# Group 0's first loads reordered and split: q first, k in two parts, key tiles cast and transposed apart, at the start of a fused attention and feed-forward kernel

## The chip, the cores and the metric

The kernel runs on one core of one Trainium2 chip. The metric is the device time of one execution in microseconds (us), the median of several runs; lower is better. Engines are named as the profile names them: PE is TensorE (matmuls; PEld are its weight loads), ACT is ScalarE, DVE is VectorE, POOL is GpSimd and SP is SyncE. POOL and SP issue the transfers (DMAs) between the chip's main memory and on-chip memory in this kernel.

## The reference

Two stages follow each other. The first is attention with a sigmoid in place of the softmax, for 8 batches of 12 heads, 448 tokens and a head size of 64. The second is a feed-forward layer with a Swish gate that has a learned slope for each hidden unit.

```python
def _attn_ref(q, k, v):                      # each (8, 12, 448, 64), float32
    S = q.shape[2]
    scale = 1.0 / np.sqrt(q.shape[-1])
    scores = scale * np.matmul(q, k.transpose(0, 1, 3, 2)) - np.log(S)
    attn = 1.0 / (1.0 + np.exp(-scores))
    return np.matmul(attn, v).astype(np.float32)

x = attn_out.transpose(0, 2, 1, 3).reshape(B * S, H * D)     # (3584, 768)

def _moe_ref(x, w_in, w_out, beta):          # w_in (768, 2048), w_out (2048, 768)
    h = x @ w_in
    g = h * (1.0 / (1.0 + np.exp(-beta * h)))
    return (g @ w_out).astype(np.float32)
```

## The kernel before

All matmuls take 16-bit operands. Heads are taken in groups of four; a batch has three groups (0, 1 and 2 make up the first batch). A group's q and k are loaded with the tokens on 128 partitions as four heads of 32 rows, and DVE's stream transposes turn them into `qT` and `kT`. A head's 448 keys fall into four key tiles: tiles 0, 1 and 2 of 128 keys and tile 3, the last, of 64.

A **visit** (`half_visit`) computes scores of one group for half of the queries (224). PE writes them to two score tiles in PSUM, and ACT turns each of the two into sigmoid weights with one instruction (`weigh`, L242). There are two kinds of visit. The first kind (`second` is 0) takes key tiles 0 and 1, and both of its score tiles are 896 wide. The second kind takes key tile 2 for all heads and then key tile 3; one of its score tiles is 896 wide, and the other, the narrow one, 448. A visit has 16 matmuls at L229; four that use different rows of the array start together. Three pairs of PSUM banks hold score tiles in turn, so a visit waits until ACT has weighed what was in its pair before. `attend` ("values", L332) multiplies the weights with v, and DVE copies the result to `xT` (L341). The first layer (`dense1`, L354) multiplies `xT` with `w_in`; ACT and DVE apply the gate (L366, L369). A unit of it is one matmul; the first 48 units take half-width operands of 224 columns, six units to each of the 16 column blocks of `w_in`, and the units behind them include full ones of 448.

All instructions stand in an order that is written out by hand. For the beginning, the list `BEGIN` holds that order: visits (`"scores"`, group, half, kind), transposes (`"k"`, `"q"`), values, units of the first layer (`"dense"`), and rows of filler matmuls (`"idle"`, L812) that multiply a tile of zeros and write to a bank that nobody reads. Each engine takes its own share of the list strictly in this order.

Two queues load the first data. SP issues group 0's k and the first half of its q, in 32-bit form, into a staging area (L787), and then `beta`. The staged parts are cast to 16 bits: k's first 8 of 14 chunks by DVE (L798), the other 6 and q by ACT (L796). POOL issues all other loads (L125, L154, L169, L177), which cast while they move: group 1's q, group 1's k, group 2's k and q, four parts of v, the other halves of q, and then `w_in` in eight parts, in the order of the list `LOADS`. From its ninth load on, a load of POOL waits until the one eight places before it has landed.

In `BEGIN`, group 0 starts like this: all of k cast, q cast, all of k transposed in two instructions (L212), q transposed (L200), group 1's q transposed, 20 fillers, the visit of the second kind, 4 fillers, the visit of the first kind. The two transposes of k cover all its key tiles: one takes row blocks 0 and 1 (four key tiles), the other row blocks 2 and 3 (three key tiles).

Of the kernel before, what the change touches and what calls it, by code (L numbers as in the profile page):

```python
# [9 lines left out]
FP16 = mybir.dt.float16  # L10
# [3 lines left out]
def kernel(  # L14
# [42 lines left out]
    kTp = ctx.enter_context(tc.tile_pool(name="kTp", bufs=3))  # L57
# [60 lines left out]
    raws = {}  # L118
# [64 lines left out]
    kT = {}  # L183
    at_tiles = {}
    xTs = {}
    ready = set()


    def in_order(b: int, t):
        t = t.rearrange("p c e -> p (c e)").bitcast(FP32)  # L190
        return t.rearrange("p (q c) -> p c q", c=NB) if b == B - 1 else t

    def transpose(g: int, r: int, c0: int = 0, c1: int = NB):
        raw = raws[g][:, r]
        assert g or (r, c0) == (0, NB // 2) or all((r, "cast", c) in ready for c in range(c0, c1))
        if r == 0:
            if g not in qT:
                qT[g] = qTp.tile([P, NB * BLK, PAIR], FP16, tag="qT", name="qT")
            ready.update((g, "q", c) for c in range(c0, c1, NB // 2))
            nc.vector.transpose(  # L200
                out=in_order(g // QPB, qT[g][:, c0 * BLK : c1 * BLK]),
                in_=raw[:, c0:c1].rearrange("p c d -> p (c d)").bitcast(FP32),
            )
            return
        ready.add((g, "k"))
        kT[g] = kTp.tile([P, S, PAIR], FP16, tag="kT", name="kT")
        to = kT[g].rearrange("p k e -> p (k e)").bitcast(FP32)
        frm = raw.rearrange("p c d -> p (c d)").bitcast(FP32).rearrange("p (c f) -> p c f", c=NB)
        half = to.rearrange("p (x i q) -> p x i q", i=2, q=BLK)
        for i in (0, 2):  # L210
            c, n = rows_of(i)
            nc.vector.transpose(  # L212
                out=half[:, i // 2 :: 2].rearrange("p j i q -> p i j q"),
                in_=frm[:, c : c + 2 * n].rearrange("p (i j) f -> p i j f", j=n),
            )

    def score_tile():
        i, j = scored[n_sc[0] % len(scored)]
        n_sc[0] += 1
        width[i] = width[j] = S  # L220
        return ps[:, i : j + 1]

    def score(sco, u0: int, s: int, jt: int, hh: int, e: int, c0: int, n: int):
        g, lo = s // 2, (s % 2 * 2 + hh) * BLK
        assert (g, "k") in ready and all(
            (g, "q", c) in ready for c in range(c0 // BLK, (c0 + n) // BLK, NB // 2)
        )
        base, nk = (last_base(s), KL) if jt == JF else (0, P)
        nc.tensor.matmul(  # L229
            sco[base : base + nk, hh, u0 : u0 + n],  # L230
            kT[g][lo : lo + BLK, jt * P : jt * P + nk, e],
            qT[g][lo : lo + BLK, c0 : c0 + n, e],
            start=(e == 0),
            stop=(e == PAIR - 1),
            tile_position=(lo, base),
        )
# [3 lines left out]
    def weigh(sco, n: int):  # L240
        slot = at_free.pop(0)
        nc.scalar.activation(  # L242
            out=attns[:, slot, :, 0:n],
            in_=sco[:, :, 0:n],
            func=AF.Sigmoid,
            bias=nlogs[:, 0:1],
            scale=MSCALE,
        )
        return slot
# [41 lines left out]

    def half_visit(g: int, c0: int, second: int):
        slots = (2 * g, 2 * g + 1)
        scos = [score_tile() for _ in slots]
        plan = [(s, jt, sco, jt * QH) for jt in (0, 1) for s, sco in zip(slots, scos)]
        widths = [S, S]
        if second:
            plan = [(s, 2, sco, 0) for s, sco in zip(slots, scos)]
            plan += [(s, JF, scos[0], QH) for s in slots]
            widths = [S, QH]  # L300
        for i in range(0, len(plan), 2):
            for e in range(PAIR):
# [447 lines left out]
    def fill_units(n: int):  # L750
        for _ in range(n):
            fill[at_fill[0]][1]()
            at_fill[0] += 1

    NH = NB // 2
    share_psum(3)
    with tc.manual_schedule():
        def load(what, *a):
# [23 lines left out]
        ]  # L782
        staged = gt[:, 0:4].rearrange("p c w -> p (c w)").bitcast(FP32)
        raws[0] = rawp.tile([P, 2, NB, D], FP16, tag="raw", name="raw")
        parts = {1: (staged, NB), 0: (staged[:, NB * D :], NH)}
        for r, (to, n) in parts.items():
            nc.sync.dma_start(  # L787
                out=to[:, 0 : n * D],
                in_=(q, k)[r][0, 0:HQ].rearrange("h (p c) d -> (h p) (c d)", c=NB)[:, 0 : n * D],
            )  # L790

        def cast(r: int, c0: int, c1: int, act: bool):
            out = raws[0][:, r, c0:c1].rearrange("p c d -> p (c d)")
            frm = parts[r][0][:, c0 * D : c1 * D]
            if act:
                nc.scalar.copy(out=out, in_=frm)  # L796
            else:
                nc.vector.tensor_copy(out=out, in_=frm)  # L798
            ready.update((r, "cast", c) for c in range(c0, c1))

        nc.gpsimd.memset(nlogs, NEG_LOG_S)
        nc.gpsimd.memset(dummy, 0.0)
# [5 lines left out]
        idle = bank(512)  # L808
# [13 lines left out]
        def beta_columns():  # L822
# [16 lines left out]
        for what, *a in BEGIN:  # L839
            if what == "q":  # L840
                g, half = a
                transpose(g, 0, half * NH, (half + 1) * NH)
            elif what == "k":
                transpose(a[0], 1)
            elif what == "scores":
                half_visit(a[0], a[1] * QH, a[2])
            elif what == "cast":
                cast(*a)
            elif what == "idle":
                idle_units(a[0])  # L850
            elif what == "v":
                double_v_last(a[0])
            elif what == "values":
                attend(a[0], a[1] * QH, QH, a[2:] or (0, 1))
            elif what == "dense":
                fill_units(a[0])
            elif what == "beta":
                beta_columns()
            elif what == "loads":
                loads()  # L860
            elif what == "two":
                share_psum(2)
# [156 lines left out]
```

## Time and profile before

| what | value |
|---|---|
| median of 3 runs | 373.51 us (373.1 to 373.65) |
| the profiled execution | 372.95 us |
| its span, first to last instruction | 371.2 us |
| mean granted PE clock | 0.999 |
| full clock granted from | 5.40 us |
| PE busy | 365.5 us (98%) |
| ACT busy | 259.7 us (70%) |
| DVE busy | 254.4 us (69%) |
| mean busy share of the 16 DMA engines | 80% or more in the first 9 of 40 slices of the span, less behind |

The profile comes from one execution. Times in it count from its first instruction. The timeline gives the start, the duration and the engine of merged instructions, with the number of them behind an "x"; a merged row's duration reaches from the first start to the last end. Brackets tell how long the engine was idle before and what ended it. A load's landing is the time at which its semaphore tells of its end. The chain is followed back from the last instruction, at each step to what released it. These landings are read from the trace:

| load | issued | landed |
|---|---|---|
| group 0's k (SP) | 0.74 | 3.90 |
| group 0's q, first half (SP) | 1.17 | 4.46 |
| beta (SP) | 1.64 | 5.54 |
| group 1's q, first half | 1.29 | 5.97 |
| group 1's k | 2.00 | 7.21 |
| group 2's k | 2.53 | 8.45 |
| group 2's q, first half | 3.05 | 9.14 |
| v, last of four parts | 5.41 | 12.79 |
| w_in, first part | 9.43 | 16.74 |
| w_in, fourth part | 12.17 | 23.66 |

### The profile page before, as it was taken

Reading aid. Unit: us, or ns where it says so; the run is one execution under the profiler, and the core shown is the slowest. Engines: PE = TensorE matmul, PEld = TensorE weight load, DVE = VectorE, ACT = ScalarE, POOL = GpSimd, SP = SyncE. Lnnn points to the kernel's source line nnn. Section 1 sums busy time; section 2 is a strip of 40 time slices with the busy share of each in tenths; the row PEclk is TensorE's granted clock in tenths of the full one; section 3 lists DMA queues with packets and bytes.
Section 4 is the critical chain, followed back from the end, with each engine's and each line's share of the span. In section 5 each row is a group of like instructions: output and inputs, shape, how many; then the busy total and the mean of one; then the engine's idle time right before and its main releaser. Section 6 shows DMA issues by size and latency. Waiting matters only on the chain.

```text
span 371.2 us, 7295 instructions
## 1 busy us (share of the span) xinstructions
PE 365.5 (98%) x2906; PEld 184.6 (50%) x2906; DVE 254.4 (69%) x479; ACT 259.7 (70%) x311; POOL 80.5 (22%) x120
## 2 busy tenths in 40 slices
PE   8999999999999999999999999999999999999997
PEld 4566544443444455544444445554444455555665
DVE  4435796777496967787666667778767667679671
ACT  5995766798967668887877749887678647883000
POOL 7732431221131013233131003233100002230000
PEclk9999999999999999999999999999999999999999
DMA  9999999893368030029829410017803111000334
GB/s 173 195 197 204 202 205 206 193 123 51 51 86 174 1 87 1 2 49 130 171 37 212 106 25 20 3 29 110 171 2 85 44 44 42 1 2 1 87 85 129
DMA packets 36226, 34.65 MB, mean 93 GB/s; under 512 B 9424, under 2 KB 32608, under 8 KB 36192
## 3 DMA queue, kind: packets, MB, share of 16 engines
q0 software_dynamic: 30288, 22.47, 42.3%
q1 hardware_dynamic: 5904, 11.71, 11.1%
q8 instruction: 23, 0.38, 0.4%
q14 instruction: 11, 0.09, 0.1%
HBM read 45.62 MB, written 11.01 MB: 153 GB/s over the span
## 4 chain that ended last, share of the span: by engine, by line
PE 93%; ACT 5%; issue 1%; DVE 0%; ACTq 0%
PE ps L643 27%; PE ps L523 26%; PE ps L229 11%; PE ps L332 10%; PE ps L354 9%; PE ps L384 4%; PE ps L437 4%; ACT attns L242 3%; ACT attns L257 1%; PE ps L812 1%; ACT sg L366 1%; DVE gt L369 0%; ACT osb L664 0%; DVE still L806 0%; ACT osb L399 0%
## 5 line engine op out<-in xcount | busy, mean ns | idle before, releaser
L257 ACT ACTIVATE attns<-ps,nlogs 128x1792 f16<-128x1792 f32 x75 | 131.7, 1756 | 41.1 <-PE ps L229 41.0
L643 PEld LDWEIGHTS <-sum 128*128 128x128 f16 x440 | 40.5, 98 | 37.3 <-issue 12.5
L537 POOL TENSOR_TENSOR gt<-attns,sg 128x448 f16<-128x448 f32 x21 | 23.9, 1137 | 141.7 <-ACT sg L534 141.7
L229 PE MATMUL ps<-qT,kT 32*128 32x448 f16 (+3 forms) x864 | 52.3, 339 | 1.1 <-ACT attns L242 0.6
L534 ACT ACTIVATE sg<-ps,beta_sb 128x448 f32<-128x448 f32 x72 | 45.2, 632 | 8.4 <-PE ps L523 5.9
L523 PE MATMUL ps<-xT,w_in 128*128 128x448 f16 x216 | 49.2, 353 | 0.0
L523 PE MATMUL ps<-xT,w_S 128*128 128x448 f16 x216 | 49.2, 352 | 0.0
L643 PE MATMUL ps<-w_T,sum 128*128 128x384 f16 x264 | 48.7, 327 | 0.0
L537 DVE TENSOR_TENSOR gt<-ps,sg 128x448 f16<-128x448 f32 x72 | 44.2, 618 | 4.0 <-ACT sg L534 3.8
L341 DVE CAST xT<-ps 128x448 f16<-128x448 f32 (+1 forms) x54 | 28.8, 567 | 21.5 <-PE ps L332 21.5
L523 PEld LDWEIGHTS <-w_in 128*128 128x128 f16 x288 | 28.0, 98 | 26.6 <-issue 0.7
L661 DVE TENSOR_TENSOR osb<-ps,osb 128x384 f32<-128x384 f32 x55 | 30.5, 554 | 15.1 <-PE ps L643 12.8
L332 PE MATMUL ps<-attns,v 128*64 128x448 f16 (+3 forms) x432 | 40.4, 340 | 0.1
L354 PE MATMUL ps<-xT,w_in 128*128 128x448 f16 (+1 forms) x240 | 39.5, 316 | 0.6 <-DVE gt L369 0.6
L630 DVE TENSOR_TENSOR sum<-gt 128x1024 f16<-128x1024 f16 x55 | 36.5, 678 | 0.2
L369 DVE TENSOR_TENSOR gt<-ps,sg 128x448 f16<-128x448 f32 (+1 forms) x40 | 20.0, 527 | 22.4 <-ACT sg L366 22.3
L125 POOL DMA_DIRECT2D raw<-in_q_dram x26 | 14.4, 555 | 92.8 <-DVE kT L212 84.7
L643 PE MATMUL ps<-w_out,gt 128*128 128x384 f16 x176 | 33.3, 327 | 0.0
L643 PE MATMUL ps<-w_out,sum 128*128 128x384 f16 x176 | 32.3, 327 | 0.0
L583 DVE TENSOR_TENSOR ps<-ps,attns 128x448 f32<-128x448 f32 x24 | 15.2, 632 | 23.3 <-PE ps L523 19.4
L523 PEld LDWEIGHTS <-w_S 128*128 128x128 f16 x216 | 21.1, 98 | 19.4
L354 PEld LDWEIGHTS <-w_in 128*128 128x128 f16 x240 | 22.0, 98 | 16.9 <-issue 5.8
(52 smaller groups left out, 364.3 us busy)
## 6 DMA issues: line engine op xcount, KB each, us to landing
out_dram<-osb SPq DMA_DIRECT2D x100, 96.0 KB, 2.2
raw<-in_k_dram POOLq DMA_DIRECT2D x23, 224.0 KB, 5.3
raw<-in_q_dram POOLq DMA_DIRECT2D x21, 224.0 KB, 4.1
v<-in_v_dram POOLq DMA_DIRECT2D x16, 192.0 KB, 6.9
w_in<-in_moe_w_in_dram POOLq DMA_DIRECT2D x8, 384.0 KB, 11.9
w_out<-in_moe_w_out_dram POOLq DMA_DIRECT2D x4, 768.0 KB, 15.0
v<-in_v_dram POOLq DMA_DIRECT2D x16, 144.0 KB, 7.5
out_dram<-osb SPq DMA_DIRECT2D x5, 144.0 KB, 2.4
```

The source lines that it names most:

```text
L229: nc.tensor.matmul(sco[base : base + nk, hh, u0 : u0 + n], kT[g][lo : lo + BLK, jt * P : jt * P + nk, e], qT[g][lo : lo + BLK, c0 : c0 + n ...
L257: nc.scalar.activation(out=attns[:, slot : slot + 2].rearrange("p n h s -> p (n h) s"), in_=sco, func=AF.Sigmoid, bias=nlogs[:, 0:1], scal ...
L332: nc.tensor.matmul(av[hh * D : (hh + 1) * D, 0:n], vs[b][base : base + nk, 2 * (s % NPAIR) + hh, jt], at[base : base + nk, hh, 0:n], start ...
L341: nc.vector.tensor_copy(out=xTs[b][:, s % NPAIR, c0 : c0 + n], in_=av[:, 0:n])
L354: nc.tensor.matmul(m1, w_in16[:, hc, dc * P : (dc + 1) * P], xTs[b][:, hc, c0 : c0 + n], start=(hc == 0), stop=(hc == NHC - 1),)
L369: nc.vector.tensor_tensor(out=gt[:, dc, off : off + n], in0=m1, in1=sg[:, 0:n], op=ALU.mult)
L523: nc.tensor.matmul(out, w[:, c, i * P : (i + 1) * P], m[:, c], start=(start and c == 0), stop=(c == KH - 1), skip_group_check=not start,)
L534: nc.scalar.activation(out=sg, in_=h, func=AF.Sigmoid, bias=0.0, scale=beta_sb[:, dc : dc + 1])
L537: return lambda: engine.tensor_tensor(out=gt[:, dc, b % 2 * S : b % 2 * S + S], in0=h, in1=sg, op=ALU.mult)
L630: nc.vector.tensor_tensor(out=sums[t, i], in0=x, in1=y, op=op)
L643: nc.tensor.matmul(m2, (x if op is None else sums[t, i])[:, dc], w[:, dc], start=first, stop=(dc == ND - 1), skip_group_check=i >= 4,)
L661: nc.vector.tensor_tensor(out=out, in0=in0, in1=in1, op=op)
```

## The change

SP issues three loads for group 0 in place of two: the half of q first, then k's first 8 chunks, then its other 6. The casts follow key tiles: `cast_q` takes q (on ACT), and `cast_k(i, lo, hi, act)` takes key tiles `lo` to `hi` of row blocks `i` and `i + 1`. `transpose` takes a range of key tiles for k, and the score matmuls ask for their key tile only. In `BEGIN`, q is cast and transposed first; then key tiles 2 and 3 are cast (the part from k's first load by DVE, the small part from its second load by ACT) and transposed; then come 16 fillers and the visit of the second kind; then key tiles 0 and 1 are cast (by DVE) and transposed, and the visit of the first kind follows without a filler between.

A visit's `second` may be 2: its two score tiles swap places, and ACT weighs the narrow one first. This holds for group 0's and group 2's first visits of the second kind.

Rows of fillers change: 16, 11 in three rows, 8, 9 and 4 (48 in all) for 20, 4, 2, 2, 8 and 6 (42). Group 1's q is transposed between the ks of groups 1 and 2. On POOL's queue, the second half of group 2's q moves behind three parts of `w_in`. Rows of the first layer between the visits become 9, 6, 21 and 12 units for 12, 6, 21 and 9, so that the fourth part of `w_in` is first used behind group 2's visit instead of ahead of it.

```diff
-    def transpose(g: int, r: int, c0: int = 0, c1: int = NB):
+    def transpose(g: int, r: int, c0: int = 0, c1: int = NB, tiles=(0, JF + 1)):
...
-        kT[g] = kTp.tile([P, S, PAIR], FP16, tag="kT", name="kT")
+        if g not in kT:
+            kT[g] = kTp.tile([P, S, PAIR], FP16, tag="kT", name="kT")
...
         for i in (0, 2):
             c, n = rows_of(i)
+            lo, hi = tiles[0], min(tiles[1], n)
             nc.vector.transpose(
-                out=half[:, i // 2 :: 2].rearrange("p j i q -> p i j q"),
-                in_=frm[:, c : c + 2 * n].rearrange("p (i j) f -> p i j f", j=n),
+                out=half[:, 2 * lo + i // 2 : 2 * hi - 1 + i // 2 : 2].rearrange("p j i q -> p i j q"),
+                in_=frm[:, c : c + 2 * n].rearrange("p (i j) f -> p i j f", j=n)[:, :, lo:hi],
             )
...
-        scos = [score_tile() for _ in slots]
+        scos = [score_tile() for _ in slots][:: -1 if second == 2 else 1]
...
-            ats = {id(sco): weigh(sco, n) for sco, n in zip(scos, widths)}
+            order = list(zip(scos, widths))[:: -1 if second == 2 else 1]
+            ats = {id(sco): weigh(sco, n) for sco, n in order}
...
         LOADS = [
-            ("q", 1, 0), ("k", 1), ("k", 2), ("q", 2, 0), ("v", 0, 3), ("q", 1, 1), ("q", 0, 1),
-            ("q", 2, 1), ("w_in", 0, 2), ("w_in", 2, 4), ("w_in", 4, 6), ("w_in", 6, 8), ("w_in", 8, 10),
-            ("w_in", 10, 12), ("w_in", 14, 16), ("w_in", 12, 14),
+            ("q", 1, 0), ("k", 1), ("k", 2), ("q", 2, 0), ("v", 0, 3), ("q", 1, 1), ("q", 0, 1), ("w_in", 0, 2),
+            ("w_in", 2, 4), ("w_in", 4, 6), ("q", 2, 1), ("w_in", 6, 8), ("w_in", 8, 10), ("w_in", 10, 12),
+            ("w_in", 14, 16), ("w_in", 12, 14),
         ]
...
-        parts = {1: (staged, NB), 0: (staged[:, NB * D :], NH)}
-        for r, (to, n) in parts.items():
+        parts = {1: staged, 0: staged[:, NB * D :]}
+        cut = 2 * rows_of(0)[1]
+        for r, c0, c1 in ((0, 0, NH), (1, 0, cut), (1, cut, NB)):
             nc.sync.dma_start(
-                out=to[:, 0 : n * D],
-                in_=(q, k)[r][0, 0:HQ].rearrange("h (p c) d -> (h p) (c d)", c=NB)[:, 0 : n * D],
+                out=parts[r][:, c0 * D : c1 * D],
+                in_=(q, k)[r][0, 0:HQ].rearrange("h (p c) d -> (h p) (c d)", c=NB)[:, c0 * D : c1 * D],
             )
...
+        def cast_k(i: int, lo: int, hi: int, act: bool):
+            c, n = rows_of(i)
+            out = raws[0][:, 1, c : c + 2 * n].rearrange("p (i j) d -> p i j d", j=n)
+            frm = parts[1][:, c * D : (c + 2 * n) * D].rearrange("p (i j d) -> p i j d", j=n, d=D)
+            copied(out[:, :, lo:hi], frm[:, :, lo:hi], act)
...
         BEGIN = [
-            ("cast", 1, 0, 8, False), ("cast", 1, 8, 14, True), ("cast", 0, 0, 7, True), ("k", 0), ("q", 0, 0),
-            ("q", 1, 0), ("idle", 20), ("scores", 0, 0, 1), ("idle", 4), ("scores", 0, 0, 0), ("k", 1),
-            ("idle", 2), ("k", 2), ("q", 2, 0), ("idle", 2), ("scores", 1, 0, 0), ("beta",), ("idle", 8),
-            ("scores", 1, 0, 1), ("v", 0), ("idle", 6), ("scores", 2, 0, 0), ("values", 0, 0), ("q", 1, 1),
-            ("scores", 2, 0, 1), ("q", 0, 1), ("values", 1, 0), ("scores", 0, 1, 0),
-            ("values", 2, 0), ("scores", 0, 1, 1), ("dense", 12), ("scores", 1, 1, 1), ("two",), ("dense", 6),
-            ("scores", 1, 1, 0), ("loads",), ("q", 2, 1), ("dense", 21), ("scores", 2, 1, 0), ("dense", 9),
-            ("values", 0, 1), ("scores", 2, 1, 1), ("values", 1, 1), ("values", 2, 1), ("dense", 39), ("k", 3),
-            ("q", 3, 0), ("q", 3, 1), ("dense", 45),
+            ("cq", 0, 7, True), ("q", 0, 0), ("ck", 0, 2, 4, False), ("ck", 2, 2, 3, True), ("k", 0, 2, 4),
+            ("idle", 16), ("scores", 0, 0, 2), ("ck", 2, 0, 2, False), ("ck", 0, 0, 2, False), ("k", 0, 0, 2),
+            ("scores", 0, 0, 0), ("k", 1), ("idle", 4), ("idle", 4), ("q", 1, 0), ("k", 2), ("idle", 3),
+            ("scores", 1, 0, 0), ("q", 2, 0), ("idle", 8), ("scores", 1, 0, 1), ("beta",), ("idle", 9),
+            ("v", 0), ("scores", 2, 0, 0), ("idle", 4), ("values", 0, 0), ("q", 1, 1), ("scores", 2, 0, 2),
+            ("q", 0, 1), ("values", 1, 0), ("scores", 0, 1, 0), ("values", 2, 0), ("scores", 0, 1, 1),
+            ("dense", 9), ("scores", 1, 1, 1), ("two",), ("dense", 6), ("scores", 1, 1, 0), ("loads",),
+            ("q", 2, 1), ("dense", 21), ("scores", 2, 1, 0), ("dense", 12), ("values", 0, 1),
+            ("scores", 2, 1, 1), ("values", 1, 1), ("values", 2, 1), ("dense", 39), ("k", 3), ("q", 3, 0),
+            ("q", 3, 1), ("dense", 45),
         ]
```

More of the change, by code (lines that the diff above doesn't have):

```diff
@@ L191, in in_order @@
         return t.rearrange("p (q c) -> p c q", c=NB) if b == B - 1 else t
-    def transpose(g: int, r: int, c0: int = 0, c1: int = NB):
+    def transpose(g: int, r: int, c0: int = 0, c1: int = NB, tiles=(0, JF + 1)):
         raw = raws[g][:, r]
-        assert g or (r, c0) == (0, NB // 2) or all((r, "cast", c) in ready for c in range(c0, c1))
+        assert g or r == 1 or c0 or all((r, "cast", c) in ready for c in range(c0, c1))
         if r == 0:
@@ L204, in transpose @@
             return
-        ready.add((g, "k"))
-        kT[g] = kTp.tile([P, S, PAIR], FP16, tag="kT", name="kT")
+        if g not in kT:
+            kT[g] = kTp.tile([P, S, PAIR], FP16, tag="kT", name="kT")
+        ready.update((g, "k", j) for j in range(*tiles))
         to = kT[g].rearrange("p k e -> p (k e)").bitcast(FP32)
@@ L211, in transpose @@
             c, n = rows_of(i)
+            lo, hi = tiles[0], min(tiles[1], n)
+            assert g or all((1, "cast", i, j) in ready for j in range(lo, hi))
             nc.vector.transpose(
-                out=half[:, i // 2 :: 2].rearrange("p j i q -> p i j q"),
-                in_=frm[:, c : c + 2 * n].rearrange("p (i j) f -> p i j f", j=n),
+                out=half[:, 2 * lo + i // 2 : 2 * hi - 1 + i // 2 : 2].rearrange("p j i q -> p i j q"),
+                in_=frm[:, c : c + 2 * n].rearrange("p (i j) f -> p i j f", j=n)[:, :, lo:hi],
             )
@@ L224, in score @@
         g, lo = s // 2, (s % 2 * 2 + hh) * BLK
-        assert (g, "k") in ready and all(
+        assert (g, "k", jt) in ready and all(
             (g, "q", c) in ready for c in range(c0 // BLK, (c0 + n) // BLK, NB // 2)
@@ L784, with copied @@
         raws[0] = rawp.tile([P, 2, NB, D], FP16, tag="raw", name="raw")
-        parts = {1: (staged, NB), 0: (staged[:, NB * D :], NH)}
-        for r, (to, n) in parts.items():
+        parts = {1: staged, 0: staged[:, NB * D :]}
+        cut = 2 * rows_of(0)[1]
+        for r, c0, c1 in ((0, 0, NH), (1, 0, cut), (1, cut, NB)):
             nc.sync.dma_start(
-                out=to[:, 0 : n * D],
-                in_=(q, k)[r][0, 0:HQ].rearrange("h (p c) d -> (h p) (c d)", c=NB)[:, 0 : n * D],
-            )
-        def cast(r: int, c0: int, c1: int, act: bool):
-            out = raws[0][:, r, c0:c1].rearrange("p c d -> p (c d)")
-            frm = parts[r][0][:, c0 * D : c1 * D]
+                out=parts[r][:, c0 * D : c1 * D],
+                in_=(q, k)[r][0, 0:HQ].rearrange("h (p c) d -> (h p) (c d)", c=NB)[:, c0 * D : c1 * D],
+            )
+        def copied(out, frm, act: bool):
             if act:
@@ L798, in cast, with cast_q @@
                 nc.vector.tensor_copy(out=out, in_=frm)
-            ready.update((r, "cast", c) for c in range(c0, c1))
+        def cast_q(c0: int, c1: int, act: bool):
+            out = raws[0][:, 0, c0:c1].rearrange("p c d -> p (c d)")
+            copied(out, parts[0][:, c0 * D : c1 * D], act)
+            ready.update((0, "cast", c) for c in range(c0, c1))
+        def cast_k(i: int, lo: int, hi: int, act: bool):
[3 more added lines that the diff above has]
+            copied(out[:, :, lo:hi], frm[:, :, lo:hi], act)
+            ready.update((1, "cast", i, j) for j in range(lo, hi))
         nc.gpsimd.memset(nlogs, NEG_LOG_S)
@@ L843 @@
             elif what == "k":
-                transpose(a[0], 1)
+                transpose(a[0], 1, tiles=tuple(a[1:]) or (0, JF + 1))
             elif what == "scores":
                 half_visit(a[0], a[1] * QH, a[2])
-            elif what == "cast":
-                cast(*a)
+            elif what == "cq":
+                cast_q(*a)
+            elif what == "ck":
+                cast_k(*a)
             elif what == "idle":
```

## The prediction

> **What bounds the kernel now.** The page comes first: the groups of engines, then the chain that ended last.
>
> ```profile
> PE 365.5 (98%) x2906; PEld 184.6 (50%) x2906; DVE 254.4 (69%) x479; ACT 259.7 (70%) x311; POOL 80.5 (22%) x120
> PE 93%; ACT 5%; issue 1%; DVE 0%; ACTq 0%
> ```
>
> TensorE (PE) carries 93% of the chain, ScalarE (ACT) 5%. The change touches only the beginning, so I asked for busy time in three stretches.
>
> ```profile
> core 0: us, PE busy (x) PEld busy (x) DVE busy (x) ACT busy (x) POOL busy (x), PEclk, DMA share, GB/s
> 0.00:6.30 6.30, 5.11 (x37) 3.27 (x38) 2.25 (x7) 2.56 (x4) 5.14 (x15) 1.00 0.74 168
> 6.30:29.50 23.20, 21.65 (x343) 14.16 (x343) 10.16 (x32) 22.38 (x30) 12.27 (x17) 1.00 1.42 194
> 29.50:371.20 341.70, 338.71 (x2532) 167.14 (x2528) 242.01 (x441) 234.71 (x277) 63.13 (x89) 1.00 0.48 85
> ```
>
> From 6.3 to 29.5 us ACT is busy 22.38 of 23.20 us: its sigmoids on scores pace that stretch, and PE's busy time there holds 22 filler matmuls. After 29.5 PE never idles for more than 0.07 us at once (gaps of 0.17 us in all). So what reaches PE's first full-width matmul of the first layer (at 29.48) earlier ends the kernel earlier by as much, if its loads are there. The start in order of time, by the timeline:
>
> ```profile
> 0.74 0.38 SPq L787 DMA_DIRECT2D gt<-in_k_dram  x1
> 1.17 0.42 SPq L787 DMA_DIRECT2D gt<-in_q_dram  x1
> 1.19 4.39 PE L812 MATMUL ps<-still 128*128 128x256 f16 x20 [1.19 <-DVE still L806]
> 3.92 1.13 ACT L796 CAST raw<-gt 128x384 f16<-128x384 f32 x2 [1.69 <-DMA gt<-in_k_dram]
> 3.92 0.56 DVE L798 CAST raw<-gt 128x512 f16<-128x512 f32 x1 [2.66 <-DMA gt<-in_k_dram]
> 4.51 0.70 DVE L212 STREAM_TRANSPOSE kT<-raw 128x256 f32<-128x256 f32 x2
> 5.14 0.37 DVE L200 STREAM_TRANSPOSE qT<-raw 128x224 f32<-128x224 f32 x1
> 5.56 0.70 PE L229 MATMUL ps<-qT,kT 32*128 32x224 f16 x16
> 6.32 13.59 ACT L242 ACTIVATE attns<-ps,nlogs 128x896 f16<-128x896 f32 x16 [1.27 <-PE ps L229]
> 7.23 0.71 DVE L212 STREAM_TRANSPOSE kT<-raw 128x256 f32<-128x256 f32 x2 [0.82 <-DMA raw<-in_k_dram]
> 13.08 0.99 PE L332 MATMUL ps<-attns,v 128*64 128x224 f16 x16
> ```
>
> k lands, is cast, transposed, then q is transposed last, PE scores, and ACT begins at 6.32. It runs nearly without a gap from there.
>
> **The start, step by step.** Group 0's bytes stay the same (672 KB in three loads for two), so the last part of k lands about when the last load lands now: q, at 4.46. I take 4.5. Bounds: 4.2, and 4.9 if a third load costs as much as a third issue (0.42). q alone should land between 3.0 (the 192 KB store takes 3.0 from issue, a 128 KB one 1.8) and 3.9 (k's 448 KB); its cast (0.57, the 448-wide one) and transpose (0.37) are done by 4.9 even at 3.9, so q leaves the path. Behind k's last part:
> - ACT's cast of 128x128: rows of 384 and 448 take 0.512 and 0.566 us, so about 0.30 (bounds 0.2 and 0.51).
> - DVE's transpose of one key tile, 128x64: 0.20 (bounds 0.15; 0.34 of the 192-wide).
> - two hand-overs of about 0.03: 4.50 + 0.02 + 0.30 + 0.03 + 0.20 + 0.04 = 5.09 for PE's first score, against 5.56.
> - The first narrow tile needs 8 matmuls, not 16. At the warm spacing (four start together, 0.1 us apart) they take 0.3; at the slow clock, at which they may still run, 0.45. ACT starts at 5.09 + 0.45 + 0.02 = 5.56, against 6.32: **0.76 earlier**.
>
> ACT then needs 0.68 for the narrow tile and 0.91 for each wide one (start to start in the trace). The remaining casts (two of 256 wide, 0.3 to 0.4 each) and transposes (0.25 each) of tiles 0 and 1 are DVE work behind the first one; they end at 6.0 to 6.4, PE scores until 6.9, ACT is busy until 5.56 + 0.68 + 0.91 = 7.15. Hidden, with 0.25 to spare. That is also what weighing the narrow tile first buys: it covers the second half of its own visit.
>
> **Where the gain meets loads.** Next visit: group 1's k lands at 7.21 as before (nothing ahead of it on POOL's queue changes). Transposes 0.63, q's 0.41 (now between the two ks; its load landed at 5.97), so PE scores from 8.29 to 8.80. ACT is free at 7.15 + 2 x 0.91 = 8.97: still 0.73 earlier than 9.70. Group 2's k lands at 8.45 and its q is transposed by 9.6, scored first at 11.7: no wait. Fillers rise from 42 to 48 in number, but each row behind the first stands before a visit that waits for a load or for ACT anyway; PE's fourth and fifth visits are ready at 10.70 and 12.30, ACT free at 10.78 and 12.37.
>
> Then `values(0, 0)` needs all four parts of v. The last lands at 12.79, 0.29 us before its use at 13.08 now. With the change PE is there at 12.83, so it starts at about 12.87. From here PE's chain is on the path: 0.91 for values, 0.63 for the next visit's issue, 0.91 for `values(1, 0)` and 0.51 + 0.02 for the visit after: ACT goes on at 15.84, against 16.50. **0.66 is left.** The later ACT work up to the last narrow tile is the same eight short sigmoids and the same visits, only moved by three units of the first layer; I cost that at nothing.
>
> One more load is near: w_in's fourth part lands at 23.66, and its first use is PE's unit 37. Before, that stood ahead of group 2's last first-kind visit, at about 23.8; the change puts the visit first, and the unit would start at 23.78. So q's second half of group 2, moved behind three w_in loads on POOL's queue (these land about 0.58 earlier, 112 KB at 194 GB/s), costs nothing: it lands near 20.5 and is transposed at 21.7. `beta` lands some 0.4 later than 5.54 and is wanted after 9.4.
>
> Sum on the profiled execution: 372.95 (span 371.20, 1.75 around it) - 0.65 = 372.30. That execution lies 0.56 below the median of the runs shown, 373.51.
>
> **The clock, weighed.** The first 20 fillers take 4.39 us (0.22 each); 8 later ones take 1.05 (0.13 each), and the trace grants full clock from 5.40 us on. The change shortens the first row to 16 fillers, ending near 4.8, and leaves PE idle for some 0.3 us before its scores. If the full clock comes in a run at 6 to 7.5 us instead of 5.40, the first visit of before runs slow: three steps of 0.1 us between its groups of four double, 0.3 later, of which ACT's small later waits (0.06, 0.05, 0.06) take up half, so it loses 0.15. The change's first visit is already priced slow. So over runs with such a spread the gain is 0.65 to 0.8. I take 0.75: 373.51 - 0.75 = 372.75. The Trainium skill ("TensorE: Matmul & The Clock Gate", Part 1) says that the full clock follows a busy window of about 3.4 us whose phase is free-running. The trace agrees as far as it goes: one grant, 4.2 us after the first filler. By that rule 16 fillers (3.5 us) fill such a window only in some phases, which speaks against this change and is the second rival.
>
> **Rivals.**
> 1. *Loads cap it.* Both margins behind the 0.66 are about 0.1 us. If v's last part or w_in's fourth lands later by 0.3 us, the gain is 0.65 - 0.2 to 0.3 = 0.4; by 0.6, nothing to 0.2. For it: DMA share 1.42 in this stretch, every load queued, k's cut adding packets. Against: the same bytes in the same order ahead of v. Time 373.1 to 373.5.
> 2. *PE stays at the slow clock; slower than before.* Price: while the clock is half, PE's work from 8.3 us on (visits, values, fillers, with hardly any idle) takes twice as long, so a grant at T loses about (T - 8.3)/2, less the 0.65. Even at 8.8 us; over 0.75 us lost from 11 us; at 12.2 us 1.95 - 0.65 = 1.3 lost: 374.8. For it: the shorter first row, and PE's idle stretch of 0.2 to 0.3 us before 8.29, after 11 fillers, which waits for group 1's k. Against: PE idles only about 0.3 us of the 4.2 us before 5.40, and in the trace of before idle stretches of 0.37 and 0.27 us (7.0, 8.7) did not lose the clock.
> 3. *The order isn't kept*: a third load lands last at 5.0 or the small copies cost their upper bounds (0.51, 0.34 and 0.4 us): PE at 5.6, ACT at 6.1, gain 0.2 to 0.3: 373.2. It counts with the first.
>
> **How the numbers follow.** A measurement of this kernel tells 0.2% (0.75 us) from no change. My forecast, the earlier start passed on to the end, has a chance of 0.65; its centre stands at that bound, and runs with a late clock are on the far side of it, so 0.50 faster and 0.15 within. Rivals 1 and 3 together 0.15, within. Rival 2 has 0.20: 0.18 slower, 0.02 within. Faster 0.50, same 0.32, slower 0.18. The range: below, the whole 0.76, the 0.3 of a slow first visit and 0.3 of measuring (half the 0.55 between the runs shown), 372.1; above, rival 2 with a grant just past 11 us, 374.2. It leaves out some 0.15 of rival 2 and a little below. The forecast's own range is 372.2 to 373.1.
>
> **What would show it.** Right: ACT's first sigmoid is a 448-wide one at about 5.55; ACT has no wait over 0.15 us up to 13 us; `values(0, 0)` starts within 0.1 us of v's landing; the first full-width matmul of the first layer stands near 28.85 (29.48 now); after it PE's gaps stay under 0.3 us in all. Wrong: that matmul near 29.5 with PE waiting for v or w_in (rival 1); fillers after 6 us still 0.2 us apart, or visits that take 0.9 us of PE (rival 2); the last part of k after 4.9 (rival 3).

## The result: slower by 1.0%

The changed kernel takes **377.3 us** (median of 6 runs, 376.36 to 377.84) where the kernel before takes 373.37 (6 runs, 373.1 to 373.65) on the same chip: a ratio of 1.0101, with a 95% interval of 1.009 to 1.0112. The forecast was 372.75, in a range of 372.1 to 374.2. The profiled execution of after took 377.84, with a span of 376.10, against 372.95 and 371.20 before. Ratios are worked out from all executions but those in a slower state of the chip (the eleventh of run 5, 381.91), so they are not quite the quotients of the medians.

The page of after: the engines' groups, then the chain that ended last.

```profile
PE 367.5 (98%) x2912; PEld 185.6 (49%) x2912; DVE 254.5 (68%) x483; ACT 259.4 (69%) x311; POOL 80.7 (21%) x120
PE 93%; ACT 3%; DMA 2%; issue 1%; DVE 0%; SPq 0%; ACTq 0%
```

The totals hardly move, but DMA stands in the chain with 2%, where it did not stand before. Busy time by stretch (columns as before; the first full-width matmul of the first layer is at 34.02 now, 29.48 before, and the last two stretches meet there):

```profile
core 0: us, PE busy (x) PEld busy (x) DVE busy (x) ACT busy (x) POOL busy (x), PEclk, DMA share, GB/s
0.00:6.30 6.30, 3.60 (x16) 2.26 (x16) 1.30 (x5) 2.05 (x3) 5.10 (x14) 1.00 0.66 138
6.30:34.00 27.70, 25.18 (x368) 16.23 (x368) 11.24 (x37) 22.82 (x31) 13.58 (x19) 1.00 1.38 196
34.00:376.10 342.10, 338.70 (x2532) 167.13 (x2528) 242.00 (x441) 234.48 (x277) 62.06 (x87) 1.00 0.46 83
```

The last stretch is 342.1 us long against 341.7, with the same 2532 matmuls. So of the 4.9 us that the span gained, 4.54 stand ahead of that matmul. The cause lies in the start; here is its timeline in after:

```profile
0.74 0.38 SPq L792 DMA_DIRECT2D gt<-in_q_dram  x1
1.17 0.89 SPq L792 DMA_DIRECT2D gt<-in_k_dram  x2
1.19 3.60 PE L827 MATMUL ps<-still 128*128 128x256 f16 x16 [1.19 <-DVE still L821]
3.36 0.56 ACT L799 CAST raw<-gt 128x448 f16<-128x448 f32 x1 [1.13 <-DMA gt<-in_q_dram]
...
4.58 0.31 DVE L215 STREAM_TRANSPOSE kT<-raw 128x128 f32<-128x128 f32 x1
7.84 0.30 ACT L799 CAST raw<-gt 128x128 f16<-128x128 f32 x1 [3.91 <-DMA gt<-in_k_dram]
8.17 0.25 DVE L215 STREAM_TRANSPOSE kT<-raw 128x64 f32<-128x64 f32 x1 [3.28 <-ACT raw L799]
8.47 2.23 PE L232 MATMUL ps<-qT,kT 32*128 32x224 f16 x32 [3.68 <-DVE kT L215]
9.08 3.39 ACT L245 ACTIVATE attns<-ps,nlogs 128x448 f16<-128x448 f32 x4 [0.94 <-PE ps L232]
10.63 2.53 PE L827 MATMUL ps<-still 128*128 128x256 f16 x11
13.09 0.88 PE L232 MATMUL ps<-qT,kT 32*128 32x224 f16 x16
13.91 1.05 PE L827 MATMUL ps<-still 128*128 128x256 f16 x8
14.02 3.34 ACT L245 ACTIVATE attns<-ps,nlogs 128x896 f16<-128x896 f32 x4 [1.54 <-PE ps L232]
```

Two things are to be seen. First, q and k's first part are there by 3.96 and their copies are done by 4.9 (the transpose at 4.58), but ACT's cast of k's second part waits 3.91 us for its load: it landed at 7.82. Everything of the first visit stands behind it, and the first sigmoid is at 9.08 instead of 6.32: **2.76 late**. Second, the third visit's first sigmoid is at 14.02 instead of 9.70: **another 1.56**. In between stand 11 fillers that take 2.53 us, 0.22 each; the 8 after them take 1.05, 0.13 each. The trace records the full clock from 13.80 on (from 5.40 before). The chain in order of time shows both pieces on the path (start, us, what):

```profile
1.64 6.17 DMA gt<-in_k_dram
...
8.47 2.23 PE ps L232 x29
10.70 2.46 PE ps L827 x11
13.16 0.82 PE ps L232 x16
```

From there on the lateness grows by only 0.22 up to the first layer (34.02 against 29.48).

### The profile page after: what moved, and what is told of

The parts are those of the page before. It is cut to its first block, busy times and chain, and to the rows that moved or that the text cites. A ratio compares the mean times of both kernels' runs of the same rounds, so it can differ in the third digit from the quotient of the medians.

```text
span 376.1 us, 7313 instructions
## 1 busy us (share of the span) xinstructions
PE 367.5 (98%) x2912; PEld 185.6 (49%) x2912; DVE 254.5 (68%) x483; ACT 259.4 (69%) x311; POOL 80.7 (21%) x120
## 4 chain that ended last, share of the span: by engine, by line
PE 93%; ACT 3%; DMA 2%; issue 1%; DVE 0%; SPq 0%; ACTq 0%
PE ps L647 27%; PE ps L527 25%; PE ps L232 12%; PE ps L336 10%; PE ps L358 9%; PE ps L388 4%; PE ps L441 4%; DMA gt<-in_k_dram 2%; PE ps L827 1%; ACT attns L245 1%; ACT attns L260 1%; ACT sg L370 1%; SPq L792 0%; ACT osb L668 0%; DVE gt L373 0%
## 5 line engine op out<-in xcount | busy, mean ns | idle before, releaser
L527 PEld LDWEIGHTS <-w_in 128*128 128x128 f16 x288 | 28.0, 98 | 26.6 <-issue 0.7
L232 PEld LDWEIGHTS <-kT 32*128 32x128 f16 (+1 forms) x864 | 14.8, 97 | 32.2 <-issue 25.7
```

What stands on the lines that cost most here:

```text
L232: nc.tensor.matmul(sco[base : base + nk, hh, u0 : u0 + n], kT[g][lo : lo + BLK, jt * P : jt * P + nk, e], qT[g][lo : lo + BLK, c0 : c0 + n ...
L527: nc.tensor.matmul(out, w[:, c, i * P : (i + 1) * P], m[:, c], start=(start and c == 0), stop=(c == KH - 1), skip_group_check=not start,)
```

## Experiments

Theory T: the loss begins with k's second part, which lands late because SP's third load runs beside POOL's stream of loads. The rivals were the new order of bytes (q first), the slow clock by itself, and the other edits of the change.

**1. One load for k, all else as in after.**

```diff
-        for r, c0, c1 in ((0, 0, NH), (1, 0, cut), (1, cut, NB)):
+        for r, c0, c1 in ((0, 0, NH), (1, 0, NB)):
```

> The changed kernel with group 0's k in one load behind q (two SP loads in place of three; q still first). Theory T, the tail: the changed kernel loses because k's second part (1536-byte packets, first at 3.30 us, last at 7.31) runs while POOL's packets (first at 3.24) are already on the DMA engines; with two loads all packets are issued 0.5 us sooner and k lands at 4.3 to 5.0; ACT's first sigmoid at 5.6 to 6.1; full clock by 8.9 at the latest; time 372.7 to 373.6. Rival R, the order: whichever load stands behind q is caught, so k lands at 5.5 to 8 and the time is 375 to 377.5. Rival C, the clock: k lands by 5 but 16 fillers are too few, the full clock comes at 12 us or later, and the time is 374 to 375.5.

Measured: 372.96 us, ratio 1.0001 (0.999 to 1.0012). The whole k landed at 4.50, the first score stood at 5.50 and the first sigmoid at 6.12. So q's place ahead of k costs nothing, and neither do the casts by key tile: the loss of 1% goes with the third load. The eleven runs fall into two groups, 372.67 to 372.96 (six) and 373.81 to 374.44 (five). The profiled execution, at 373.81, is of the upper one, and its timeline has the second cost of after still in it: the fillers ahead of the third visit are 0.2 us apart up to 9.34, where T had the full clock by 8.9:

```profile
7.66 2.19 PE L827 MATMUL ps<-still 128*128 128x256 f16 x11
```

**2 and 6. POOL's first load issued later.** A fill on POOL ahead of its loads, of a tile that is written over later, delays its whole queue (1.38 us of fill in run 2; in run 6 the fill is twice as wide and takes 2.66).

```diff
         nc.gpsimd.memset(dummy, 0.0)
+        nc.gpsimd.memset(w_out16[:, 0:2], 0.0)     # run 6: 0:4
```

> The changed kernel with one memset on POOL (128x1536, of a part of w_out's tile that is loaded over later) ahead of POOL's first load, so that POOL's loads begin some 1 to 2 us later. Theory T: SP's three loads then end alone, k's second part lands at 4.2 to 4.8 instead of 7.82, ACT's first sigmoid comes at 5.5 to 5.9; POOL's loads land as late as in the changed kernel or up to 0.5 us later than that, so that group 1's k and v bound instead: time 374 to 376. Rival (a third SP load is slow by itself): k's second part still lands after 6.5, time 377 to 379.

> The changed kernel with a memset of 128x3072 on POOL ahead of its first load (that of 128x1536 took 1.38 us and put POOL's first packet at 3.98; this one should put it near 5.4). Theory T: k's second part, SP's third load, is late only by running beside POOL's packets; now it runs alone and lands at 4.2 to 4.8 (7.82 in the changed kernel, 6.19 with the shorter memset). Rival: a third load on SP's queue is slow by itself, and it lands after 5.8. The time (376 to 378) tells nothing, since all of POOL's loads come later.

Measured: run 2 376.06, ratio 1.0075 (1.0062 to 1.0088); run 6 374.87 in one execution. The table has what the theory speaks of, with POOL's first packet taken from the trace's packet records.

| kernel | POOL's first packet | k's second part lands | first sigmoid | third visit's first sigmoid |
|---|---|---|---|---|
| after | 3.24 | 7.82 | 9.08 | 14.02 |
| run 2 | 3.98 | 6.19 | 7.28 | 11.79 |
| run 6 | 4.82 | 5.08 | 6.34 | 11.07 |

The later POOL's stream, the earlier the third load: 2.74 us of its lateness go with it. T had 4.2 to 4.8 for both runs. In run 2 POOL's packets still came 1.8 us ahead of the load's last one (5.82), and it landed 1.4 later than T's latest. In run 6 its last packet ends at 4.77, ahead of all of POOL's, and it still lands 0.6 later than the last load of before (4.46): that is the price, in one execution, of a third load with nothing of POOL beside it, 0.3 above what T expected at most. SP's loads in the DMA view (KB of one, us from issue to landing), of after and then of run 6:

```profile
gt<-in_k_dram SPq DMA_DIRECT2D x1, 256.0 KB, 2.8
gt<-in_q_dram SPq DMA_DIRECT2D x1, 224.0 KB, 2.6
gt<-in_k_dram SPq DMA_DIRECT2D x1, 192.0 KB, 6.2
```

```profile
...
gt<-in_k_dram SPq DMA_DIRECT2D x1, 192.0 KB, 3.4
```

The first two loads take the same in both; the third, the smallest, takes 6.2 or 3.4. The mixing costs POOL's stream too: in run 2 group 1's k lands at 8.00, against 8.80 in after, though POOL issued its loads 0.83 later. Neither run mends the kernel: PE idles until its first score, the clock is slow ahead of the third visit, and run 6 issues POOL's first loads 2.1 us later, so its time (376 to 378 was expected) is no price of the load alone.

**3. The third load from another queue.** k's second part is issued by ACT, at 0.74, ahead of its table load.

```diff
-            nc.sync.dma_start(
+            (nc.scalar if c0 else nc.sync).dma_start(
                 out=parts[r][:, c0 * D : c1 * D],
```

> The changed kernel with k's second part issued from ACT's queue (ahead of its table load) instead of as SP's third load; bytes and packets as in the changed kernel. Theory T: its packets start at about 1.8 instead of 3.30 and are done before POOL's spread; k's second part lands at 3.9 to 4.6, q up to 0.6 later than 3.34, ACT's first sigmoid at 5.4 to 5.9; time 372.5 to 373.5. Rival (the number of packets and parts costs, not the time at which they start): the last of the three loads still lands after 6.5, time 376 to 378.

Measured: 374.5, ratio 1.0032 (1.002 to 1.0044). The loads land at 4.10 (q), 4.28 (k's second part, from ACT's queue) and 4.82 (k's first part), the first sigmoid is at 6.45. The load is on time as T says, but the time is 1 us above what T expected at most. What is left grows while the clock is slow: the full one is recorded from 9.18 only, and the third visit's first sigmoid stands at 10.48, 0.78 behind before, where the first one was 0.13 behind. That the clock did it is argued from these times, not shown by this run.

**7. The cut alone, in the kernel before.** Only k's load is cut, order k, k, q; no other edit.

```diff
-        for r, (to, n) in parts.items():
+        for r, c0, c1 in ((1, 0, 8), (1, 8, NB), (0, 0, NH)):
...
```

> The kernel before with one thing of the change: k's load cut in two (8 and 6 chunks), in the order k, k, q, so that q is SP's third load. Nothing else is changed. Theory T: what comes third is caught beside POOL's packets, so q lands at 6 to 8 instead of 4.46, ACT's first sigmoid comes at 7.9 to 9.8, and the time is 375 to 377.5. Rival (q first, or the small 1536-byte packets, is what made it late): q lands by 5.0 and the time is 373.0 to 373.9.

Measured: **376.89**, ratio 1.0102 (1.0089 to 1.0116): the whole loss of after, from this one edit. Now both parts of k land early, at 3.52 and 3.97, and q, which is third, lands at 7.13. Its timeline where q arrives:

```profile
7.16 0.56 ACT L796 CAST raw<-gt 128x448 f16<-128x448 f32 x1 [2.65 <-DMA gt<-in_q_dram]
7.75 0.70 DVE L200 STREAM_TRANSPOSE qT<-raw 128x224 f32<-128x224 f32 x2 [2.83 <-ACT raw L796]
...
8.22 0.70 PE L229 MATMUL ps<-qT,kT 32*128 32x224 f16 x16 [2.58 <-DVE qT L200]
```

In both orders the load that is third on SP's queue is late, be it k's second part or q.

**4. PE kept at work until k is there.** After with 46 fillers for 16.

```diff
-            ("idle", 16), ("scores", 0, 0, 2),
+            ("idle", 46), ("scores", 0, 0, 2),
```

> The changed kernel with 46 fillers in the first row instead of 16 (PE busy with zeros until about 8.4 us). k's second part still lands near 7.8 and ACT's first sigmoid comes at 8.9 to 9.1. Theory T with the clock as its consequence: the full clock comes at 5 to 8 us instead of 13.80, the 11 fillers ahead of group 1's first visit take 1.3 instead of 2.46 us, ACT's idle stretch of 1.5 us before 14.0 goes away, and the time falls by 1.2 to 2 us against the changed kernel, to 375.3 to 376.1. Rival C (the clock is the main loss): the time falls by 3 us or more, to 374.3 or less. If the slow clock costs nothing: 377 to 377.6.

Measured: 376.43, ratio 1.0079 (1.0066 to 1.0092), 0.87 below after. The full clock is recorded from 6.74, and the 11 fillers ahead of the third visit take 1.38 where they took 2.53. k's part landed at 7.49, but the fillers ran to 9.07: the first score is at 9.01, and the first sigmoid at 9.44, 0.36 later than after's. T had expected the time to fall by 1.2 to 2 us, and it fell by less. So the slow clock cost after between 0.87 and, if the 0.36 passes to the end in full, 1.2 us; the other 2.7 to 3.1 of its 3.9 are the late load.

**11. Fewer fillers ahead of the third visit.** After with 2 in place of 4 + 4 + 3.

```diff
-            ("scores", 0, 0, 0), ("k", 1), ("idle", 4), ("idle", 4), ("q", 1, 0), ("k", 2), ("idle", 3),
+            ("scores", 0, 0, 0), ("k", 1), ("idle", 2), ("q", 1, 0), ("k", 2),
```

> The changed kernel with 2 fillers instead of 11 ahead of group 1's first visit. Theory: in the changed kernel those 11 ran at the slow clock (10.63 to 13.09 us), on the path, and made ACT's idle stretch of 1.5 us before 14.0; with 2 this stretch falls below 0.4 us and the time by 0.9 to 1.5, to 375.8 to 376.5. Rival (group 1's loads, transposes or the slow clock itself hold that visit): 376.8 to 377.8.

Measured: 376.79, ratio 1.0095 (1.0081 to 1.0109), 0.51 below after by the medians and 0.81 by the profiled executions. The third visit's first sigmoid comes forward to 12.44, by 1.58, but the clock is still slow until 14.04, and at the first full-width matmul (33.16) 0.86 is left. The theory had expected 0.9 to 1.5 at the end, to 376.5 at most; the median lies at the rival's edge (376.8). Taking fillers out wins only a part: what follows them is slow as well.

**10. The shorter first row, in the kernel before.**

```diff
-            ("q", 1, 0), ("idle", 20), ("scores", 0, 0, 1), ("idle", 4), ("scores", 0, 0, 0), ("k", 1),
+            ("q", 1, 0), ("idle", 16), ("scores", 0, 0, 1), ("idle", 4), ("scores", 0, 0, 0), ("k", 1),
```

> The kernel before with 16 fillers in the first row instead of 20 and nothing else changed. Theory (a shorter row lets the full clock come a window of 3.4 us later in part of the runs): the first score starts at 5.56 as before, but the runs spread: some at 373.1 to 373.5 and some 0.4 to 1.0 us above them, median 373.3 to 374.0. Rival (the row's length does nothing by itself; only the late load made the clock slow): 373.1 to 373.6 with no group above.

Measured: 373.94 (8 runs, 373.21 to 374.84), ratio 1.0021 (1.001 to 1.0033). Busy time and granted clock (PEclk, the value behind POOL's) in four stretches of 3.41 us between the clock changes that the trace of this run records, at 3.89, 7.30 and 14.13:

```profile
0.48:3.89 3.41, 2.70 (x13) 1.94 (x14) 0.40 (x2) 1.49 (x2) 2.73 (x7) 1.00 0.59 189
3.89:7.30 3.41, 1.92 (x27) 0.96 (x25) 1.93 (x5) 1.72 (x3) 2.81 (x5) 1.00 1.05 161
7.30:10.71 3.41, 3.04 (x38) 1.62 (x36) 2.43 (x9) 2.99 (x5) 1.89 (x4) 0.50 1.36 190
10.71:14.13 3.42, 3.42 (x29) 1.76 (x28) 0.45 (x2) 2.46 (x3) 3.39 (x6) 0.50 1.41 195
```

The full clock came at 3.89 and was taken away again at 7.30, after a stretch in which PE was busy 1.92 of 3.41 us, waiting 1.49 of it for q's transpose. (In this execution k and q landed 0.37 and 0.36 later than in that of before, which is a part of the wait.) The 0.50 of the next two stretches lasts until 14.13. The phase of these stretches is not the kernel's to choose, but over eight runs the four fillers fewer cost 0.67 us, with k's load uncut.

**5. Both repairs.** After with one load for k and 20 fillers.

```diff
-        for r, c0, c1 in ((0, 0, NH), (1, 0, cut), (1, cut, NB)):
+        for r, c0, c1 in ((0, 0, NH), (1, 0, NB)):
...
-            ("idle", 16), ("scores", 0, 0, 2),
+            ("idle", 20), ("scores", 0, 0, 2),
```

> The two-load kernel (group 0's q, then k in one load) with 20 fillers in the first row instead of 16, as before the change. The two-load kernel's runs fell into two groups, 372.67 to 372.96 and 373.81 to 374.44, and its profiled run, of the upper group, had fillers 0.2 us apart until 9.2 us. Theory: the upper group is runs whose full clock comes a window late, since 16 fillers end 0.7 us before the first score; with 20 the row reaches to 5.5, the full clock comes by 7 us in nearly every run, ACT's first sigmoid at 5.9 to 6.2, and nearly all runs lie at 372.5 to 373.0. Rival: the two groups come from the landing of the loads (group 1's k at 7.2 or 7.9); then they stay, about half of the runs above 373.7.

Measured: 372.94, ratio 0.9991 (0.9982 to 1.0); ten of eleven runs lie between 372.57 and 373.49, and the upper group of run 1 is gone. In its profile the full clock is recorded from 6.91, the third visit's sigmoid is at 9.48 and the first full-width matmul at 29.50, hardly other than before (9.70 and 29.48). All the rest of the change, at best, breaks even.

**8 and 9. The narrow tile first, alone, in the kernel before.** Run 8 weighs it first in group 0's first visit; run 9 in the first visit of group 0 and both of group 2.

```diff
-        scos = [score_tile() for _ in slots]
+        scos = [score_tile() for _ in slots][:: -1 if second == 2 else 1]
...
-            ats = {id(sco): weigh(sco, n) for sco, n in zip(scos, widths)}
+            order = list(zip(scos, widths))[:: -1 if second == 2 else 1]
+            ats = {id(sco): weigh(sco, n) for sco, n in order}
...
-            ("q", 1, 0), ("idle", 20), ("scores", 0, 0, 1), ("idle", 4),
+            ("q", 1, 0), ("idle", 20), ("scores", 0, 0, 2), ("idle", 4),
```

> The kernel before with one thing of the change: group 0's first visit weighs its narrow score tile first. Theory: its first sigmoid needs 8 of 16 matmuls and comes at 5.9 to 6.0 instead of 6.32; the visits behind wait for group 1's k (7.21) and for v (12.79) with 0.1 to 0.3 us to spare, so 0.25 to 0.4 us pass to the end: 372.9 to 373.1. Rival (fillers and ACT's queue give it back): 373.2 to 373.5, not to be told from before.

> The kernel before with the narrow tile weighed first in three visits of the second kind: group 0's first, group 2's first, and group 2's second (query half 2). Loads, casts and fillers as before. Theory: each of the three stands where ACT waits for PE (0.3, 0.17 and 0.1 to 0.3 us by the traces), so the gain of the first alone (0.28) grows to 0.45 to 0.65: 372.6 to 372.9. Rival: v's landing (12.79 to 12.96) holds the middle, and it stays at 372.9 to 373.1.

Measured: run 8 372.95, ratio 0.9991 (0.9982 to 1.0), 0.28 below the kernel before on its chip; run 9 373.08, ratio 0.9994 (0.9985 to 1.0003). In run 8 the first sigmoid is at 6.00, 0.32 earlier, and the third visit's at 9.19, 0.51 earlier. Then `values(0, 0)` waits for the last part of v, which lands at 12.96:

```profile
13.10 0.99 PE L333 MATMUL ps<-attns,v 128*64 128x224 f16 x16 [0.45 <-DMA v<-in_v_dram]
```

Before, the same step stood at 13.08. So the half microsecond won ahead of it ends there, and run 8's first full-width matmul stands at 29.32, 0.16 earlier than before. In run 9 v lands at 13.25, values start at 13.38, and that matmul is at 29.48 as before; the time is the rival's (372.9 to 373.1). No kernel here beats the kernel before by more than 0.1%.

## Why the prediction was wrong

**The step that failed** is the first of "The start, step by step": "Group 0's bytes stay the same (672 KB in three loads for two), so the last part of k lands about when the last load lands now: q, at 4.46. I take 4.5. Bounds: 4.2, and 4.9 if a third load costs as much as a third issue (0.42)." It landed at 7.82. The bound took the price of one more load for the price of its issue. The runs put two other prices in its place: about 0.6 for a third load with nothing of POOL beside it (5.08 in run 6 against 4.46), and 2.7 for running beside POOL's stream. The trace of before could have raised the question: there POOL's first packets start at 3.84, and the last of the 256 packets of SP's two loads ends at 4.15, so SP's two loads were nearly alone. That nobody was beside them was a condition of the 4.46, and the cut took it away. The same sharing moved group 1's k, which the prediction kept at 7.21, to 8.80.

The Trainium skill ("DMA: Bandwidth & Descriptors", Issuing engines are not separate DMA queues) says that transfers started by different engines run on the same 16 DMA engines and interleave. The runs agree: POOL's packets, put off by 0.74 and by 1.58 us, let SP's third load through 1.63 and 2.74 us earlier. The page also says that a second issuing engine saves only issue time. Run 3 saved more than that: the load from ACT's queue was issued 0.90 earlier than as SP's third (0.74 for 1.64) and landed 3.54 earlier (4.28 for 7.82); its packets, from 2.06 to 3.79, were through ahead of POOL's first (4.01).

**Rival 2 was right as the second part.** It had a chance of 0.20 and a price of (T - 8.3)/2, with T the time of the grant, by which 13.80 costs 2.75. (Less the 0.65 this breaks even at 9.6, not at the 8.8 that the prediction gives.) The runs put the slow clock's share of after at 0.9 to 1.2. The formula takes PE's work for the bound from 8.3 us on at either clock. With the full clock it is not: in run 4 ACT's first five sigmoids follow each other without a wait, and from the first to the third visit's first it takes 3.20 us (3.38 before), against 4.94 in after. And PE waited for k until 8.47 at any clock. The rival's evidence against itself was weighed wrongly: "in the trace of before idle stretches of 0.37 and 0.27 us (7.0, 8.7) did not lose the clock". In that trace PE was busy 2.94 of the 3.41 us from 5.40 on; run 10 lost the clock with 1.92. What the runs speak for is the busy share of a whole stretch, not the length of one idle piece. The prediction also let the two costs stand as alternatives, with chances of their own. They feed each other: the late load leaves PE idle, and a PE that idles is not granted the full clock (after: 1.23 us busy in the 3.41 from 3.56 on) or loses it (run 7: 1.41). The range's upper end, 374.2, had room for a grant just past 11 us with k on time, and for no more.

**Rival 3** named a k that lands after 4.9, but priced it only to 5.0, at "gain 0.2 to 0.3". With 7.82 for 4.5 its own chain of steps puts the first sigmoid at 8.88; 9.08 was measured.

**What held.** The order of bytes: q first costs nothing (run 1). q left the path (landed at 3.34, transposed by 4.37). The small copies: ACT's 128x128 cast took 0.298 (0.30 said), the 128x64 transpose 0.246 (0.20 said), the 256-wide casts 0.25 to 0.295 (0.3 to 0.4), the 128-wide transposes 0.311 and 0.270 (0.25). The narrow sigmoid was read too long: ACT took 0.53 for it, start to start (9.08 to 9.61), and the 0.68 read in the trace of before held a wait for PE. From k's landing to the first score it was 0.65, 0.59 said; from there to the first sigmoid 0.61, 0.47 said. These steps together add 0.2 to the 3.3 of the load. The forecast that the gain would end near `values(0, 0)` and v's landing is what runs 8 and 9 show, though the cap is lower than forecast: v lands at 12.96 and 13.25, not at 12.79. And the lower group of run 1 (372.67 to 372.96), 0.36 to 0.65 below the kernel before beside it (373.32), lies where the forecast lay; that these are the runs with a full clock is argued from the profile of the upper group and from run 5, not shown, as no execution of the lower group was profiled.

**Left open.** Why a third load of SP suffers so beside POOL's stream, when the first two lose nothing (2.6 and 2.8 us in after and in run 6), the records do not tell: they give no DMA engine for a packet. They do show that the cut also brought POOL's first packets forward, from 3.84 to 3.24 (3.06 in run 7), with POOL's instructions at the same times. That moment follows SP's loads: in the eleven kernels without a fill on POOL, POOL's first packet starts 0.07 to 0.19 us ahead of the first data packet of SP's third transfer (`beta` where group 0 has two loads on SP), while the last packets of the second are still out. So POOL's stream seems to come in as SP's first two loads run out, and the cut left fewer bytes in these two (480 KB in after for 672 KB before); what holds it back until then is not shown. Of the 0.6 for a third load, the part of the different sizes and order wasn't tried apart.

## What to carry to other kernels

Cutting a load into two cost more here than one issue, because the extra load came last on its queue: look up when the other queues' first packets start, for a load that still had packets out by then shared the engines with all that followed, and expect the cut to move that moment (from 3.84 to 3.24 here). Put the bytes that start the chain into as few loads as were through before that moment, or hold the other stream back. And a row of fillers has to reach the first real work with room to spare: when a load is late, an idle PE stays at the slow clock or falls back to it, and then the later fillers, put there to cost nothing, stand on the path at twice their length.

## What was not expected of the hardware

- **The price of a place in the queue.** The same 192 KB took 2.8 us from issue to landing as SP's second load (run 7), 3.4 as its third with POOL's first packet at 4.82, 4.5 with that at 3.98, and 6.2 with it at 3.24. In the DMA view's slices of 0.4 us from 0 on, the rate of all loads in after falls from 305 GB/s to 72 as SP's second load ends, and stays under 175 to 6.8 us, while most of the third load is still to be moved. Before (second line) has 114 to 188 from 4.0 to 6.8 us as well, with the last packet of SP's two loads ending at 4.15: a late load shares a rate that is low by then:

```profile
GB/s 0 0 0 0 99 175 361 364 305 72 139 158 118 122 131 160 171 203 193 172 175 184 195 193 195 195 193 190 189 193 191 202 196 192 197 197 198 196 196 195
GB/s 0 0 0 0 99 233 358 412 354 301 165 114 125 186 188 166 184 190 179 181 167 182 187 173 188 188 183 191 193 197 203 193 202 196 194 200 228 186 188 191
```

- **The clock goes by stretches, and by how busy they are.** All the changes recorded in one trace lie a multiple of 3.41 us apart, at a phase that differs from run to run. The full clock was lost after stretches in which PE was busy 1.41 us (runs 2 and 7) and 1.92 (run 10), so with PE far from idle; it was kept after 2.94 (before) and 2.68 (run 9). Of stretches with only fillers in them, those up to 2.61 us (2.31 in run 5, 2.37 in after, 2.43 in run 3, 2.61 in run 6) granted nothing and those from 2.70 on (run 10; 2.83 in run 7, 2.99 in run 2) granted it. With the scores of 32 rows among the matmuls it is less plain: 3.04 and 3.05 (runs 10 and 7, at the slow clock) granted nothing, 3.21 (run 3) did. The Trainium skill ("TensorE: Matmul & The Clock Gate", Part 1) gives the same 3.4 us and a free-running phase, and has the clock fall back after one idle window or more; by these runs such a window may hold 1.92 us of matmuls.
- **The clock's column can hide a slow start.** The trace counts PEclk as 1.00 ahead of the first change that it records, as in after from 6.30 to 34.00, where 11 fillers ran at 0.22 us each. The spacing of like matmuls told the clock there, the column didn't.
